# One core's attention and two MoE layers: a half-size group with two column tiles in a PSUM bank, and a new order for the first 30 microseconds

## The chip, the cores and the metric

The kernel runs on one core of a Trainium2 chip. A core has a matmul engine (TensorE, PE; the loading of its stationary operand is shown as PEld), VectorE (DVE), ScalarE (ACT), GpSimd (POOL, idle here), and SyncE (SP), whose queue issues every transfer of this kernel, in order. The metric is the time of one execution on the device, in microseconds (us).

## The reference

```python
scores = scale * np.matmul(q_c, k_c.transpose(0, 1, 2, 4, 3))       # chunks of 64, 8 heads of 64
attn = np.exp(scores - np.max(scores, axis=-1, keepdims=True))
attn = attn / (np.sum(attn, axis=-1, keepdims=True) + 1e-09)
x = heads_side_by_side(np.matmul(attn, v_c))                         # 4608 tokens x 512
a = x @ w1
b = x @ w2                                                           # 512 x 1024
x = (a * b @ w3) @ w_out                                             # w3: 1024 x 1024, w_out: 1024 x 512
h = x @ w_in                                                         # 512 x 2048
g = np.maximum(h, 0.0) + alpha * np.minimum(h, 0.0)                  # one alpha per column
out = g @ w_out2                                                     # 2048 x 512
```

`heads_side_by_side` stands for the reference's transpose and reshape. The weights of the two layers come as 64-bit floating-point numbers and are converted on the chip.

## The kernel before

Each fp32 operand is split into a high and a low half (`split`, HI and LO), and each product of 128x128 by 128 x columns is three matmuls, low by high, high by high and high by low (`PASSES`).

**Beginning.** Attention goes by units of 256 tokens (u = 0 to 17), two units to a block of 512 tokens (b). A unit has the steps S (scores, 64 small matmuls), M (max, two VectorE instructions), X (16 exponentials on ScalarE, eight for each of its two tiles), Y (sums and division on VectorE), T (8 transposes), P (ScalarE's copy `pt`), V (64 small matmuls into `pa`), c and d (high half of x by ScalarE, low half by VectorE). Each piece of a weight has A (ScalarE: absolute values), B (VectorE, 3 instructions), C (ScalarE's cast `wa`), D and E (VectorE, 2 each); the transfer that brings a piece is called `raw`, and piece n + 3 is asked for when piece n is done with its buffer. `a0.0` is the first product, block 0, column tile 0 of w1; k is ScalarE's copy of it out of PSUM, b the product with w2, m the multiplication of the two on VectorE. The string `STARTUP` is the order in which these steps are written; the framework's scheduler (`tile`) sets the order on each engine from it and from its own estimates, except for instructions given to `keep_in_program_order`. `LEAD = 4` blocks are worked in this stretch, and blocks 0 and 1 take turns first. Each product uses 12 matmuls of 512 columns.

**moe2's first product.** w_in's column tiles j = 0 to 7 are multiplied by operands that stand for x's parts in a scheme of seven products in place of eight (`ORDER`, `operand`). Tokens go in groups s (`wide = [512] * 4 + [256]`): four full-size groups and one of half size, in which every tile is 256 columns wide. A pass (s, j) works on two column tiles, j and j + 1, in the banks `a` and `b`, with a third pair of banks `bc` in turn. It has 14 products of 6 matmuls, in the order 4, 5, 3, 5, 0, 2, 6, 1 with two tiles each; ScalarE copies a bank out at three of them (`keep`: p1, u2, v), VectorE adds `bc` to these, and `leaky` makes the result: two relus on ScalarE, one multiply-add with alpha on VectorE, and a store to DRAM (`g2_dram`) from the buffer `r`. All copies and results take 128x512 buffers from one pool with `TMP = 7` slots. The weights of the second product (w_out2) are loaded into the places of those of the first as these are used for the last time, by the same queue as the stores.

**moe2's second product** ("q", "a", "b" from `op`) reads `g2_dram` back; its first matmuls need the banks a and b.

Of the kernel before, what the change touches and what calls it, by code (L numbers as in the profile page):

```python
# [18 lines left out]
P = 128  # L19
# [18 lines left out]
    S0 M0 X0 A0 S1 Y0 M1 T0 P0 B0 X1 V0 D0 c0 Y1 C0 A1 d0 T1 A2 E0 P1 S2 B1  # L38
    V1 A3 c1 M2 C1 d1 X2 D1 S3 B2 a0.0 M3 C2 Y2 X3 E1 T2 D2 b0.0 B3 P2 Y3 k0.0 V2
    C3 A4 m0.0 T3 c2 E2 P3 d2 a0.1 A5 D3 B4 V3 k0.1 E3 C4 c3 D4 b0.1 A6 d3 q4 q5 E4  # L40
    a1.0 m0.1 A7 B5 a0.2 k1.0 B6 C5 D5 C6 b1.0 D6 k0.2 E5 E6 A8 b0.2 m1.0 A9 B7 a1.1 m0.2 C7 D7
    B8 a0.3 k1.1 E7 C8 D8 A10 b1.1 k0.3 B9 E8 C9 b0.3 m1.1 A11 D9 B10 a1.2 m0.3 C10 E9 a0.4 k1.2 D10
    A12 B11 b1.2 k0.4 E10 C11 D11 A13 b0.4 m1.2 E11 B12 A14 a1.3 S4 m0.4 C12 D12 a0.5 M4 B13 k1.3 X4 E12
    C13 b1.3 D13 k0.5 A15 B14 E13 b0.5 C14 m1.3 S5 D14 M5 m0.5 E14 B15 Y4 X5 C15 D15 T4 P4 E15 a1.4
    A16 B16 k1.4 b1.4 C16 D16 E16 V4 Y5 q6 m1.4 a0.6 A17 B17 k0.6 b0.6 C17 D17 E17 T5 P5 V5 q7 m0.6
    a1.5 A18 B18 k1.5 b1.5 C18 D18 E18 m1.5 a0.7 A19 B19 k0.7 b0.7 C19 D19 E19 m0.7 a1.6 A20 B20 k1.6 b1.6 C20
    D20 E20 c4 d4 c5 d5 m1.6 a1.7 A21 B21 k1.7 b1.7 C21 D21 E21 S6 M6 X6 m1.7 a2.0 A22 B22 k2.0 b2.0
    C22 D22 E22 S7 M7 Y6 X7 m2.0 a2.1 A23 B23 k2.1 b2.1 C23 D23 E23 T6 P6 V6 c6 d6 m2.1 a2.2 A24
    B24 k2.2 b2.2 C24 D24 E24 Y7 T7 P7 V7 m2.2 a2.3 A25 B25 k2.3 b2.3 C25 D25 E25 c7 d7 m2.3 h0.0 A26
    B26 C26 D26 E26 h0.1 s0 w0 A27 B27 C27 D27 E27 a2.4 A28 B28 k2.4 b2.4 C28 D28 E28 m2.4 h1.0 A29 B29  # L50
    C29 D29 E29 a2.5 A30 B30 k2.5 b2.5 C30 D30 E30 m2.5 h1.1 s1 w1 a2.6 A31 B31 k2.6 b2.6 C31 D31 E31 m2.6
    h2.0 A32 B32 C32 D32 E32 a2.7 A33 B33 k2.7 b2.7 C33 D33 E33 m2.7 h2.1 s2 w2 A34 B34 C34 D34 E34 h3.0
    A35 B35 C35 D35 E35 a3.0 A36 B36 k3.0 b3.0 C36 D36 E36 m3.0 h3.1 s3 w3 a3.1 A37 B37 k3.1 b3.1 C37 D37
    E37 m3.1 h4.0 A38 B38 C38 D38 E38 a3.2 A39 B39 k3.2 b3.2 C39 D39 E39 m3.2 h4.1 s4 w4 a3.3 k3.3 b3.3 m3.3
    h5.0 h5.1 s5 w5 a3.4 k3.4 b3.4 m3.4 h6.0 a3.5 k3.5 b3.5 m3.5 h6.1 s6 w6 a3.6 k3.6 b3.6 m3.6 h7.0 a3.7 k3.7 b3.7
    m3.7 h7.1 s7 w7
# [7 lines left out]
TMP = 7  # L64


@with_exitstack
def tile_attention_moe_moe(ctx: ExitStack, tc: tile.TileContext, qkv: bass.AP, w12: bass.AP,
# [8 lines left out]
    nc = tc.nc  # L77
    NT, DM = out.shape
# [29 lines left out]
    def matmul(*args, **kw):  # L108
        ins = nc.tensor.matmul(*args, **kw)  # L109
        if pinned[0]:  # L110
            tc.keep_in_program_order(ins)

    def transpose(*args, **kw):
        ins = nc.tensor.transpose(*args, **kw)  # L114
        if pinned[0]:
            tc.keep_in_program_order(ins)

    def split(dst, src):

        nc.scalar.copy(dst[:, HI], src)  # L120
        nc.vector.tensor_tensor(out=dst[:, LO], in0=src, in1=dst[:, HI].bitcast(F32), op=ALU.subtract)  # L121
# [39 lines left out]
    def convert_a(i):  # L161
# [22 lines left out]
    def convert_c(i):
        nc.scalar.copy(w_g[conv[i]][:, HI], conv_m[i])

    def convert_d(i):

        p = conv_p[i] = tmp("p")
        nc.vector.tensor_scalar(out=p.bitcast(U32), in0=conv_m[i].bitcast(U32), scalar1=0xFF800000, scalar2=None,  # L190
                                op0=ALU.bitwise_and)
        nc.vector.scalar_tensor_tensor(out=p, in0=conv_raw[i][:, :, 0], scalar=2.0 ** -52, in1=p, op0=ALU.mult, op1=ALU.mult)

    def convert_e(i):
        m, g = conv_m[i], w_g[conv[i]]
        nc.vector.tensor_tensor(out=m, in0=m, in1=g[:, HI].bitcast(F32), op=ALU.subtract)  # L196
        nc.vector.tensor_tensor(out=g[:, LO], in0=m, in1=conv_p[i], op=ALU.add)
# [4 lines left out]
    def second_weight(i):  # L202
# [6 lines left out]
        nc.vector.tensor_tensor(out=m, in0=m, in1=conv_p.pop(i), op=ALU.add)  # L209

    def combined_weight(i):
# [14 lines left out]
        for out, x, y in ((t14[:, left], b12, b11), (t32[:, left], b22, b12), (t32[:, right], b22, t14[:, left]),  # L226
                          (t14[:, right], b21, t32[:, right])):
            nc.vector.tensor_tensor(out=out, in0=x, in1=y, op=ALU.subtract)
# [30 lines left out]
    def load_unit(u):  # L259
# [9 lines left out]
        v = un[u]["v"]  # L269
        for j in range(2):  # L270
            nc.sync.dma_start(out=un[u]["qk"][j], in_=qkv[2 * u + j, :, 0:2])
        for j in range(2):
# [16 lines left out]
    def attn_max(u):  # L289
        mx = un[u]["mx"] = work.tile([P, 2, 8], F32, tag="mx", name="mx")  # L290
        nc.vector.tensor_reduce(out=mx, in_=un[u]["s"].rearrange("p h (a k) -> p h a k", k=D), axis=AX.X, op=ALU.max)
        nc.vector.tensor_scalar_mul(mx, mx, -SCALE)  # L292

    def attn_exp(u, tiles=range(2)):
# [4 lines left out]
        for j in tiles:  # L299
            for a in range(4):  # L300
                for h2 in range(2):
                    n, h = 4 * j + a, h2 ^ (a & 1)
                    nc.scalar.activation(out=e[:, j, a, h], in_=s[:, h2, n * D:(n + 1) * D], func=AF.Exp,  # L303
                                         bias=mx[:, h2, n:n + 1], scale=SCALE, accum_out=sm[:, j, a, h:h + 1])

    def attn_softmax(u):
        e, sm = un[u]["e"].rearrange("p j a h k -> p (j a h) k"), un[u].pop("sm").rearrange("p j a h -> p (j a h)")
        nc.vector.tensor_scalar_add(sm, sm, 1e-9)
        nc.vector.reciprocal(sm, sm)
        nc.vector.tensor_tensor(out=e, in0=e, in1=sm.unsqueeze(2).to_broadcast([P, 16, D]), op=ALU.mult)  # L310
# [8 lines left out]
    def attn_copy(u):  # L319
        pt = un[u]["pt"] = work.tile([P, 2, 4, 2, D], F32, tag="pt", name="pt", bufs=1)  # L320
        nc.scalar.copy(pt.rearrange("p j a c s -> p j (a c s)"), un[u]["pa"])
# [13 lines left out]
    def attn_out(u, lo):  # L335
# [5 lines left out]
        if lo:  # L341
            nc.vector.tensor_tensor(out=xs[LO], in0=pa, in1=xs[HI].bitcast(F32), op=ALU.subtract)  # L342
            un.pop(u)
        else:
            nc.scalar.copy(xs[HI], pa)
# [15 lines left out]
    def fold_split(f, lo):  # L361
# [3 lines left out]
        if lo:  # L365
            nc.vector.tensor_tensor(out=dst[:, LO], in0=ps, in1=dst[:, HI].bitcast(F32), op=ALU.subtract)
        else:
            nc.scalar.copy(dst[:, HI], ps)
# [6 lines left out]
    def product(b, f, a, ps):  # L375
        nc.vector.tensor_tensor(out=a, in0=ps, in1=a, op=ALU.mult)
# [5 lines left out]
    def empty_pair(sums, last, name, to):  # L382

        for i in (last - 1, last):
            t = tmp(name)
            (nc.scalar.copy if i % 2 else nc.vector.tensor_copy)(t, sums[i])
# [53 lines left out]
    def add(out, x, y, op=ALU.add):  # L440
        nc.vector.tensor_tensor(out=out, in0=x, in1=y, op=op)  # L441
# [19 lines left out]
    def operand(o):  # L461
# [9 lines left out]
        nc.scalar.copy(h, x)  # L471
# [4 lines left out]
    for u in range(4):  # L476
        load_unit(u)
        if u < RAW:
            convert_load(u)
    nc.sync.dma_start(out=alpha_sb, in_=alpha)  # L480
    nc.vector.tensor_scalar_mul(nalpha, alpha_sb, -1.0)
    lent = {1: "p23", 3: "p23", 5: "p23", 7: "p23"}
    sets = 0
    for step in STARTUP.split():
        kind, rest = step[0], [int(n) for n in step[1:].split(".")]
        n = rest[0]
        if kind == "q":
# [3 lines left out]
        elif kind in "ST":  # L491
            {"S": attn_scores, "T": attn_transpose}[kind](n, lent.get(n, "att"))
        elif kind in "MXYPV":
# [11 lines left out]
        elif kind == "k":  # L505
            a = ab[tuple(rest)][2] = tmp("a")
            nc.scalar.copy(a, ab[tuple(rest)][0])  # L507
# [9 lines left out]


# [45 lines left out]
    for b in range(LEAD, NB):  # L564
        parts = [p for i in range(2) for p in unit_steps(2 * (b + 1) + i, False)] if b + 1 < NB else []
        for f in range(NF1):
# [5 lines left out]
            nc.scalar.copy(a, pa)  # L572
# [275 lines left out]
```

## Time and profile before

| | |
|---|---|
| time, median of 3 runs | 1462.27 us (1460.94 to 1463.52) |
| profiled execution | 1463.75 us, its span 1461.9 us |
| mean granted clock of TensorE | 0.995 |
| TensorE busy | 1411.9 us (97%) |
| VectorE busy | 1001.7 us (69%) |
| ScalarE busy | 737.5 us (50%) |
| the first product starts | 37.62 us |
| the half-size group, first matmul to the next stage's first | 1054.98 to 1105.42 us |

The profiled execution's time holds some 2 us outside the span, which runs from the first to the last instruction. Busy shares are means over the whole span. An engine's line in a timeline has its start, its duration, the operation with its output and inputs, how many of a kind stand in a row, and in brackets how long the engine had been idle and what released it.

### The profile page before, as it was taken

What the parts mean: (1) busy time and instruction counts of PE and PEld (TensorE: products, weight loads), DVE (VectorE), ACT (ScalarE), POOL (GpSimd) and SP (SyncE); (2) the same over time, 40 slices, a digit from 0 to 9 for tenths busy, and PEclk for the clock granted to TensorE, in tenths of its full rate; (3) what the DMA queues carried; (4) which work ended last, traced back from release to release, by engine and by line L of the source; (5) the groups of instructions that cost most, each with busy time, mean ns of one, the idle gap of its engine ahead of it and who ended that gap; (6) DMA issues with size and microseconds to landing.
All of it is one profiled execution on the core that took longest, in us unless ns stands there. A gap on an engine that the chain in (4) does not pass through costs nothing.

```text
span 1461.9 us, 22936 instructions
## 1 busy us (share of the span) xinstructions
PE 1411.9 (97%) x8608; PEld 1167.7 (80%) x8608; DVE 1001.7 (69%) x1533; ACT 737.5 (50%) x1603; POOL 0.7 (0%) x6
## 2 busy tenths in 40 slices
PE   4999999999999999999999999999999999999998
PEld 3777788887788888888878787878787888888887
DVE  4988786233487877776345758575756878888775
ACT  5545532144355545553247767686765444444433
POOL 0000000000000000000000000000000000000000
PEclk9999999999999999999999999999999999999999
DMA  8555342344466666668272424333589563745442
GB/s 260 188 188 168 108 157 95 131 151 148 141 216 217 216 216 220 218 221 304 91 273 108 148 112 158 116 137 116 177 277 324 188 216 116 210 136 176 144 140 89
DMA packets 132095, 256.32 MB, mean 175 GB/s; under 512 B 13712, under 2 KB 62864, under 8 KB 131984
## 3 DMA queue, kind: packets, MB, share of 16 engines
q1 hardware_dynamic: 131984, 254.87, 52.0%
q8 instruction: 67, 1.10, 0.3%
q14 instruction: 44, 0.36, 0.1%
HBM read 160.44 MB, written 94.37 MB: 174 GB/s over the span
## 4 chain that ended last, share of the span: by engine, by line
PE 83%; DVE 6%; ACT 5%; DMA 4%; issue 1%; SPq 0%; ACTq 0%; DVEq 0%
PE a L109 18%; PE b L109 18%; PE q L109 17%; PE acc L109 12%; PE bc L109 8%; PE ab L109 4%; PE wc L109 3%; ACT e L303 2%; DMA g_dram<-r 2%; PE sc L109 1%; PE pa L109 1%; DMA raw<-in_w 1%; PE pa L114 1%; DVE m L181 1%; DVE m L196 1%
## 5 line engine op out<-in xcount | busy, mean ns | idle before, releaser
L109 PE MATMUL q<-op,w 128*128 128x512 f32 (+1 forms) x1020 | 220.5, 369 | 2.2 <-DVE op L441 2.1
L109 PE MATMUL acc<-gs,wc 128*128 128x512 f32 x864 | 207.9, 393 | 3.4 <-DVE gs L121 3.1
L109 PEld LDWEIGHTS q<-op,w 128*128 128x128 f32 x1020 | 179.4, 190 | 34.4 <-DVE op L441 2.6
L109 PEld LDWEIGHTS acc<-gs,wc 128*128 128x128 f32 x864 | 160.3, 188 | 40.7 <-DVE gs L121 5.2
L109 PE MATMUL a<-x,wa 128*128 128x512 f32 x672 | 165.1, 394 | 0.4 <-DVE x L342 0.4
L109 PE MATMUL b<-x,wa 128*128 128x512 f32 x672 | 163.9, 392 | 0.0
L109 PEld LDWEIGHTS a<-x,wa 128*128 128x128 f32 x672 | 127.1, 190 | 27.1 <-DVE x L342 0.5
L109 PEld LDWEIGHTS b<-x,wa 128*128 128x128 f32 x672 | 124.8, 188 | 25.8
L109 PE MATMUL bc<-yo,w 128*128 128x512 f32 (+1 forms) x600 | 134.6, 368 | 0.0
L658 ACT CAST op<-araw 128x1024 fp32r<-128x1024 f32 (+1 forms) x80 | 77.3, 967 | 94.4 <-PE q L109 33.1
L109 PEld LDWEIGHTS bc<-yo,w 128*128 128x128 f32 x600 | 105.5, 189 | 18.7
L109 PE MATMUL b<-yo,w 128*128 128x512 f32 (+1 forms) x450 | 105.3, 369 | 1.7 <-ACT t L606 1.4
L441 DVE TENSOR_TENSOR op<-araw,op 128x1024 fp32r<-128x1024 f32 (+1 forms) x80 | 88.8, 1112 | 21.1 <-ACT op L658 20.5
L109 PE MATMUL ab<-x,wa 128*128 128x512 f32 x384 | 96.4, 400 | 4.9 <-ACT a L507 4.9
L109 PE MATMUL a<-yo,w 128*128 128x512 f32 (+1 forms) x390 | 92.1, 372 | 7.3 <-ACT p L619 5.0
L303 ACT ACTIVATE e<-sc,mx 128x64 f32<-128x64 f32 x288 | 86.2, 351 | 21.8 <-DVE mx L292 21.0
L109 PEld LDWEIGHTS b<-yo,w 128*128 128x128 f32 x450 | 79.1, 188 | 17.4 <-ACT t L606 3.0
L658 ACT CAST op<-sum 128x1024 fp32r<-128x1024 f32 (+1 forms) x60 | 58.0, 967 | 64.8 <-PE q L109 48.2
L109 PEld LDWEIGHTS ab<-x,wa 128*128 128x128 f32 x384 | 71.5, 190 | 23.2 <-ACT a L507 8.4
L109 PEld LDWEIGHTS a<-yo,w 128*128 128x128 f32 x390 | 68.3, 188 | 23.1 <-ACT p L619 6.6
L441 DVE TENSOR_TENSOR op<-sum,op 128x1024 fp32r<-128x1024 f32 (+1 forms) x60 | 66.6, 1109 | 28.1 <-ACT op L658 28.1
L303 ACT ACTIVATION_READ_ACCUMULATOR e<-sc,mx 128x1 f32 x288 | 70.1, 244 | 0.0
(121 smaller groups left out, 2075.6 us busy)
## 6 DMA issues: line engine op xcount, KB each, us to landing
araw<-g_dram SPq DMA_DIRECT2D x80, 512.0 KB, 3.9
g_dram<-r SPq DMA_DIRECT2D x128, 256.0 KB, 2.0
w_dram<-wm SPq DMA_DIRECT2D x48, 512.0 KB, 2.9
w<-w_dram SPq DMA_DIRECT2D x48, 512.0 KB, 4.9
qk<-in_qkv SPq DMA_DIRECT2D x36, 512.0 KB, 5.8
raw<-in_w2nd SPq DMA_DIRECT2D x32, 512.0 KB, 4.2
y_dram<-y SPq DMA_DIRECT2D x36, 256.0 KB, 2.8
raw<-in_w SPq DMA_DIRECT2D x16, 512.0 KB, 4.2
```

Source lines behind the costliest of these rows:

```text
L109: ins = nc.tensor.matmul(*args, **kw)
L114: ins = nc.tensor.transpose(*args, **kw)
L181: nc.vector.scalar_tensor_tensor(out=m.bitcast(U32), in0=conv_raw[i][:, :, 1], scalar=0xC0000000, in1=m.bitcast(U32), op0=ALU.bitwise_and, ...
L196: nc.vector.tensor_tensor(out=m, in0=m, in1=g[:, HI].bitcast(F32), op=ALU.subtract)
L303: nc.scalar.activation(out=e[:, j, a, h], in_=s[:, h2, n * D:(n + 1) * D], func=AF.Exp, bias=mx[:, h2, n:n + 1], scale=SCALE, accum_out=sm ...
L441: nc.vector.tensor_tensor(out=out, in0=x, in1=y, op=op)
L658: ins = nc.scalar.copy(out, x)
```

## The change

Two things. First, in the half-size group a pass works on four column tiles and not on two: each of the banks a, b and bc takes two tiles of 256 columns side by side, the group has two passes and not four, and copies, relus, adds and stores are 512 wide; the multiply-add with alpha stays 256 wide, since alpha differs by tile. Second, the beginning: q and k of units 0 and 1 and the first two weight pieces are asked for first, then v of these units, and after them the rest; an exponential on a single zero runs ahead of everything; the negated alpha is computed at the end of the beginning; and up to the mark `|` in `STARTUP`, which stands behind the first product, the three computing engines keep the written order (`InOrder`, `head`).

```diff
 STARTUP = """
-    S0 M0 X0 A0 S1 Y0 M1 T0 P0 B0 X1 V0 D0 c0 Y1 C0 A1 d0 T1 A2 E0 P1 S2 B1
+    S0 A0 M0 X0 B0 D0 S1 M1 C0 X1.0 Y0 A1 X1.1 E0 T0 B1 D1 P0 V0 Y1 c0 T1 C1 d0
...
+class InOrder:
+    def __init__(self, tc, engine, on):
+        self.tc, self.engine, self.on = tc, engine, on
+
+    def __getattr__(self, name):
+        f = getattr(self.engine, name)
+
+        def call(*args, **kw):
+            ins = f(*args, **kw)
+            if self.on[0]:
+                self.tc.keep_in_program_order(ins)
+            return ins
+        return call
...
+    head = [False]
+    vector, scalar = InOrder(tc, nc.vector, head), InOrder(tc, nc.scalar, head)
...
-        if pinned[0]:
+        if pinned[0] or head[0]:
             tc.keep_in_program_order(ins)
...
-    for u in range(4):
+    vector.memset(nalpha[:, 0:1], 0.0)
+    scalar.activation(out=nalpha[:, 0:1], in_=nalpha[:, 0:1], func=AF.Exp)
+    for u in range(2):
+        load_unit(u, False)
+        convert_load(u)
+    for u in range(2):
+        load_values(u)
+    convert_load(2)
+    for u in range(2, 4):
         load_unit(u)
-        if u < RAW:
-            convert_load(u)
     nc.sync.dma_start(out=alpha_sb, in_=alpha)
-    nc.vector.tensor_scalar_mul(nalpha, alpha_sb, -1.0)
+    head[0] = True
...
-    def leaky(s, j, q, h, t):
-        w, f = wide[s], j + NJ * (q % 2)
-        r = tmp("r")[:, :w]
-        nc.scalar.activation(out=r, in_=h, func=AF.Relu)
-        nc.scalar.activation(out=t, in_=h, func=AF.Relu, scale=-1.0)
-        nc.vector.scalar_tensor_tensor(out=r, in0=t, scalar=nalpha[:, f:f + 1], in1=r, op0=ALU.mult, op1=ALU.add)
-        nc.sync.dma_start(out=g2_dram[s, q, j // 2][:, j % 2], in_=r)
+    def leaky(s, js, q, h, t):
+        w, r = wide[s], tmp("r")[:, :h.shape[1]]
+        scalar.activation(out=r, in_=h, func=AF.Relu)
+        scalar.activation(out=t, in_=h, func=AF.Relu, scale=-1.0)
+        for i, j in enumerate(js):
+            f, at = j + NJ * (q % 2), slice(i * w, (i + 1) * w)
+            vector.scalar_tensor_tensor(out=r[:, at], in0=t[:, at], scalar=nalpha[:, f:f + 1], in1=r[:, at],
+                                           op0=ALU.mult, op1=ALU.add)
+        j = js[0]
+        to = g2_dram[s, q, j // 2]
+        nc.sync.dma_start(out=to[:, j % 2] if len(js) == 1 else to, in_=r if len(js) == 1 else r.rearrange("p (j c) -> p j c", j=2))
...
+    passes = []
+    for s, w in enumerate(wide):
+        n = TB // w
+        passes += [(s, j, [list(range(j + i * n, j + (i + 1) * n)) for i in range(2)]) for j in range(0, NJ, 2 * n)]
...
+        def both(i, o, ps, first, last):
+            w = wide[s]
+            for n, k in enumerate(jj[i]):
+                product(s, k, o, ps[:, n * w:(n + 1) * w], first and n == 0, last)
...
         for i in range(2):
-            product(s, jj[i], 4, a[i], True, False)
+            both(i, 4, a[i], True, False)
             p1[i] = keep("p1", i)
```

The other products of a pass change in the same way as the last one shown. What the change moves on the engines stands in their rows. First ScalarE, from the start of the program; before:

```order
L303 ACT_TABLE_LOAD
L303 ACTIVATE e,sm<-sc,mx 128x64 x16
L172 ACTIVATE m<-raw 128x512
L321 COPY pt<-pa 128x1024
L303 ACTIVATE e,sm<-sc,mx 128x64 x16
L345 CAST x<-pa 128x2x2x256
L185 CAST wa<-m 128x512
L172 ACTIVATE m<-raw 128x512 x2
L321 COPY pt<-pa 128x1024
L185 CAST wa<-m 128x512 x2
L303 ACTIVATE e,sm<-sc,mx 128x64 x3
L345 CAST x<-pa 128x2x2x256
```

and now:

```order
L77 ACT_TABLE_LOAD
L77 ACTIVATE nalpha<-nalpha 128x1
L77 ACTIVATE m<-raw 128x512
L77 ACTIVATE e,sm<-sc,mx 128x64 x16
L77 CAST wa<-m 128x512
L77 ACTIVATE e,sm<-sc,mx 128x64 x8
L77 ACTIVATE m<-raw 128x512
L77 ACTIVATE e,sm<-sc,mx 128x64 x8
L77 COPY pt<-pa 128x1024
L77 CAST x<-pa 128x2x2x256
L77 CAST wa<-m 128x512
L77 COPY pt<-pa 128x1024
```

The table load stands ahead of an exponential that needs no data, the first weight piece ahead of unit 0's exponentials, a weight's cast and its next piece ahead of and between unit 1's exponentials, and the first of unit 2's exponentials (the row x3 of before) no longer ahead of the high half of unit 1's x; they come four rows further on. TensorE from the start of the program (L109 and L114, and now L128 and L133, are the lines of the helpers for matmuls and transposes); before:

```order
L109 MATMUL sc<-qk 64x64 x64
L114 MATMUL pa<-ident,e 128x128 x8
L109 MATMUL pa<-pt,v 64x64 x32
L114 MATMUL pa<-ident,e 128x128 x8
L109 MATMUL sc<-qk 64x64 x32
L109 MATMUL pa<-pt,v 64x64 x32
L109 MATMUL sc<-qk 64x64 x32
L109 MATMUL a<-x,wa 128x512 x12
L109 MATMUL b<-x,wa 128x512 x6
```

and now:

```order
L128 MATMUL sc<-qk 64x64 x64
L133 MATMUL pa<-ident,e 128x128 x8
L128 MATMUL pa<-pt,v 64x64 x32
L133 MATMUL pa<-ident,e 128x128 x8
L128 MATMUL pa<-pt,v 64x64 x32
L128 MATMUL sc<-qk 64x64 x32
L128 MATMUL a<-x,wa 128x512 x12
L128 MATMUL sc<-qk 64x64 x32
```

The scores of unit 3 (the last `sc` row) stand behind the first product and no longer ahead of it, and both values steps ahead of unit 2's scores. Last, TensorE at the start of the half-size group; before:

```order
L109 MATMUL a<-yo,w_6802 128x256 x6
L109 MATMUL b<-yo,w_6880 128x256 x6
L109 MATMUL bc<-yo,w_6802 128x256 x6
L109 MATMUL a<-yo,w_6800 128x256 x6
L109 MATMUL b<-yo,w_6878 128x256 x6
L109 MATMUL bc<-yo,w_6880 128x256 x6
L109 MATMUL a<-yo,w_6798 128x256 x6
L109 MATMUL b<-yo,w_6876 128x256 x6
L109 MATMUL bc<-yo,w_6800 128x256 x6
```

and now:

```order
L128 MATMUL a<-yo,w_6804 128x256 x6
L128 MATMUL a<-yo,w_6882 128x256 x6
L128 MATMUL b<-yo,w_7215 128x256 x6
L128 MATMUL b<-yo,wx 128x256 x6
L128 MATMUL bc<-yo,w_6804 128x256 x6
L128 MATMUL bc<-yo,w_6882 128x256 x6
L128 MATMUL a<-yo,w_6802 128x256 x6
L128 MATMUL a<-yo,w_6880 128x256 x6
L128 MATMUL b<-yo,w_7213 128x256 x6
```

Each bank now takes 12 matmuls with two tiles' weights where it took 6, and comes round again after six rows and not after three.

## Rows read from the trace of the kernel before

**Rows 1.** Page, part 1: busy time and share of the span of each engine.

```profile
PE 1411.9 (97%) x8608; PEld 1167.7 (80%) x8608; DVE 1001.7 (69%) x1533; ACT 737.5 (50%) x1603; POOL 0.7 (0%) x6
```

**Rows 2.** Stretches: length, each engine's busy time, granted clock, DMA share, GB/s.

```profile
37.60:60.00 22.40, 21.77 (x215) 17.39 (x212) 20.03 (x38) 15.74 (x55) 0.00 (x0) 0.90 0.68 213
1035.94:1054.98 19.04, 19.04 (x85) 15.77 (x84) 14.48 (x22) 16.50 (x30) 0.00 (x0) 1.00 0.60 209
1054.98:1105.42 50.44, 43.96 (x337) 40.98 (x335) 30.60 (x63) 33.89 (x91) 0.00 (x0) 1.00 0.85 279
```

**Rows 3.** TensorE's timeline, first 58 us: start, duration, operation, idle before and releaser.

```profile
4.58 2.35 PE L109 MATMUL sc<-qk 64*64 64x64 f32 x64 [4.58 <-DMA qk<-in_qkv]
...
26.19 1.94 PE L114 MATMUL pa<-ident,e 128*128 128x128 f32 x8 [4.61 <-DVE e L310]
...
29.82 1.93 PE L109 MATMUL pa<-pt,v 64*64 64x64 f32 x64
35.70 1.99 PE L109 MATMUL sc<-qk 64*64 64x64 f32 x64 [3.95 <-DVE x L342]
37.62 5.00 PE L109 MATMUL a<-x,wa 128*128 128x512 f32 x12
...
52.44 3.02 PE L109 MATMUL ab<-x,wa 128*128 128x512 f32 x12
...
56.11 2.11 PE L109 MATMUL a<-x,wa 128*128 128x512 f32 x8 [0.39 <-DVE x L342]
```

**Rows 4.** ScalarE's timeline, first 58 us, same columns.

```profile
8.51 1.28 ACT L303 ACT_TABLE_LOAD   x1 [8.51 <-DVE mx L292]
...
14.45 0.75 ACT L172 ACTIVATE m<-raw 128x512 f32<-128x512 f32 x1
...
24.08 1.11 ACT L345 CAST x<-pa 128x1024 fp32r<-128x1024 f32 x1
...
28.22 1.01 ACT L321 COPY pt<-pa 128x1024 f32<-128x1024 f32 x1 [1.39 <-PE pa L114]
...
40.13 0.31 ACT L303 ACTIVATE e<-sc,mx 128x64 f32<-128x64 f32 x1 [1.29 <-DVE mx L292]
```

**Rows 5.** VectorE's timeline, first 58 us, same columns.

```profile
8.25 0.17 DVE L292 TENSOR_SCALAR mx<-mx 128x16 f32<-128x16 f32 x1
...
47.93 0.69 DVE L192 SCALAR_TENSOR_TENSOR p<-raw,p 128x512 f32<-128x512 uint32 x1
...
54.84 1.22 DVE L342 TENSOR_TENSOR x<-pa,x 128x1024 fp32r<-128x1024 f32 x1
```

**Rows 6.** TensorE's timeline in the half-size group.

```profile
1059.23 0.98 PE L109 MATMUL a<-yo,w 128*128 128x256 f32 x6 [1.94 <-ACT p L619]
...
1074.05 0.88 PE L109 MATMUL a<-yo,w 128*128 128x256 f32 x6
1074.77 0.88 PE L109 MATMUL b<-yo,w 128*128 128x256 f32 x6
...
1105.42 0.96 PE L109 MATMUL a<-op,w 128*128 128x512 f32 x3 [1.26 <-ACT t L606]
```

**Rows 7.** ScalarE's waits in the half-size group: total us, times, longest.

```profile
ACT v L619 <- DMA g_dram<-r: 3.1, 4, 1.3
```

**Rows 8.** ScalarE by shape, half-size group: busy us, mean ns, idle before.

```profile
L605 ACT ACTIVATE r<-p 128x256 f32<-128x256 f32 x8 | 3.3, 418 | 5.6 <-DVE p L441 5.3 <-DVE r L607 0.3
...
L619 ACT COPY p<-a 128x256 f32<-128x256 f32 x4 | 1.4, 351 | 0.0
```

**Rows 9.** The same of full-size groups, 960 to 1050 us.

```profile
L605 ACT ACTIVATE r<-p 128x512 f32<-128x512 f32 x10 | 6.3, 632 | 10.2 <-DVE p L441 10.0
...
L619 ACT COPY p<-a 128x512 f32<-128x512 f32 x5 | 2.9, 581 | 0.0
```

**Rows 10.** DMA issues in the half-size group: KB each, median us to landing.

```profile
w<-w_dram SPq DMA_DIRECT2D x13, 512.0 KB, 4.6
g_dram<-r SPq DMA_DIRECT2D x28, 128.0 KB, 3.4
```

More of the change, by code (lines that the diff above doesn't have):

```diff
@@ L208, in second_weight @@
         m = conv_m[i]
-        nc.vector.tensor_tensor(out=m, in0=m, in1=conv_p.pop(i), op=ALU.add)
+        vector.tensor_tensor(out=m, in0=m, in1=conv_p.pop(i), op=ALU.add)
     def combined_weight(i):
@@ L341, in attn_out @@
         if lo:
-            nc.vector.tensor_tensor(out=xs[LO], in0=pa, in1=xs[HI].bitcast(F32), op=ALU.subtract)
+            vector.tensor_tensor(out=xs[LO], in0=pa, in1=xs[HI].bitcast(F32), op=ALU.subtract)
             un.pop(u)
         else:
-            nc.scalar.copy(xs[HI], pa)
+            scalar.copy(xs[HI], pa)
     wc_g = {}
@@ L385, in empty_pair @@
             t = tmp(name)
-            (nc.scalar.copy if i % 2 else nc.vector.tensor_copy)(t, sums[i])
+            (scalar.copy if i % 2 else vector.tensor_copy)(t, sums[i])
             nc.sync.dma_start(out=to(i), in_=t)
@@ L470, in operand @@
         y_op[s, o] = h, l
-        nc.scalar.copy(h, x)
+        scalar.copy(h, x)
         add(l, x, h.bitcast(F32), ALU.subtract)
@@ L484, in tile_attention_moe_moe @@
     for step in STARTUP.split():
-        kind, rest = step[0], [int(n) for n in step[1:].split(".")]
-        n = rest[0]
-        if kind == "q":
+        kind, rest = step[0], [int(n) for n in step[1:].split(".") if n]
+        n = rest[0] if rest else 0
+        if kind == "|":
+            head[0] = False
+        elif kind == "q":
             load_unit(n)
@@ L492, in tile_attention_moe_moe @@
             {"S": attn_scores, "T": attn_transpose}[kind](n, lent.get(n, "att"))
+        elif kind == "X" and len(rest) > 1:
+            attn_exp(n, rest[1:])
         elif kind in "MXYPV":
@@ L506, in tile_attention_moe_moe @@
             a = ab[tuple(rest)][2] = tmp("a")
-            nc.scalar.copy(a, ab[tuple(rest)][0])
+            scalar.copy(a, ab[tuple(rest)][0])
         elif kind == "b":
@@ L617, in keep @@
         def keep(name, i):
-            t = tmp(name)[:, :w]
-            nc.scalar.copy(t, a[i])
+            t = tmp(name)
+            scalar.copy(t, a[i])
             return t
         def second(i):
-            n = 4 * NJ * s + j + i
-            bc = pair(("att", "p01", "p23")[n % 3], "bc")
-            b[i], c[i] = (bc[:, h, :w] for h in range(2))
-            product(s, jj[i], 5, b[i], True, True)
+            bc = pair(("att", "p01", "p23")[(2 * turn + i) % 3], "bc")
+            b[i], c[i] = (bc[:, h] for h in range(2))
@@ L657, in copied @@
     def copied(out, x):
-        ins = nc.scalar.copy(out, x)
+        ins = scalar.copy(out, x)
         if ordered[0]:
```

116 lines of the change are left out of this document (60 added, 56 removed).

## The prediction, on record before the changed kernel ran

> **What bounds the kernel now.** I read the page first: TensorE is busy 97% of the span [rows 1], so only places where it waits or runs slowly can give time back. I then took TensorE's waits and cut the span where they lie: the first 56 us, and the 50.44 us of the half-size group (the last 256 columns of moe2's first product). The full-size pass just before that group has no wait at all: 19.04 us long, TensorE busy 19.04 [rows 2]. That is 14 banks of six 512-column matmuls, 1.36 us each.
>
> In the half-size group the reader should see two things. A bank of six 256-column matmuls costs 0.72 us when nothing stalls (1074.05 to 1074.77) [rows 6], and there are 4 passes x 14 = 56 of them, so the matmuls alone are 40.32 us; the group takes 50.44 [rows 2]. The missing 10.1 us is waiting, named in the rows as "a <- ACT p" (1.94 at the first) and "a <- ACT t" (1.26 at the end) [rows 6]: TensorE wants to write a bank again, and ScalarE has not copied it out. ScalarE is not slow for want of rate: a copy of 256 columns costs 0.351 us and one of 512 costs 0.581, a relu 0.418 against 0.632 [rows 8, 9]. Most of the price of the narrow ones is paid per instruction. Per 256-column pass ScalarE has 6 copies and 16 relus, 6 x 0.351 + 16 x 0.418 = 8.8 us, against 10.08 us of matmuls: it fits on average, but not within the 2.16 us that three banks leave it.
>
> At the beginning TensorE waits for the first attention units. ScalarE stands idle until 8.51, loads its activation table for 1.28 us and only then starts the first exponentials [rows 4]. The scores of unit 3, which themselves waited 3.95 us for VectorE, and most of unit 2's exponentials stand ahead of the first product, which starts at 37.62 and needs 5.00 us for twelve matmuls, where a later set needs 3.02 [rows 3]. The granted clock of 37.6 to 60 is 0.90 [rows 2], so part of this stretch ran at the lower of its two levels (1.2 against 2.4 GHz). The next block's first product begins at 56.11, 0.39 us late, on VectorE's x [rows 3]. From there TensorE is fed well, and I count the beginning's gain at that point.
>
> **The half-size group, part by part.** Two column tiles share a bank, so the matmuls stay (336 of 128x256) and 2 passes of 14 double banks, 1.44 us each, replace 4 of 14: the floor stays 2 x 14 x 1.44 = 40.32 us. ScalarE's work per pass becomes 6 x 0.581 + 16 x 0.632 = 13.6 us [rows 9] against 20.16 us of matmuls, 67%; in the full-size pass, which has the same instructions, it is 13.6 of 19.04, or 71%, and TensorE does not wait there [rows 2]. The adds on VectorE halve in number; its multiply-adds with alpha stay 256 wide. So the pace should be that of the full-size pass, a little slacker.
>
> What is left over: at the entry the bank "a" is wanted again after three double banks, 4.32 us instead of 2.16, at about 1059.30, and the copy that TensorE waits for ended just before 1059.23 today [rows 6], because ScalarE is still working off the full-size pass. I take 0.2. At the exit the next product waits 1.26 for the last relu [rows 6]; the wider relus come later after their bank but TensorE also writes more after it, so I keep 1.26. Sum 41.8.
>
> The transfers: with the DMA share 0.85 over 50.44 us [rows 2], the queues hold 42.9 us of work, which is more than 41.8. The stores become 16 of 256 KB instead of 32 of 128 KB (28 of which are issued inside the stretch [rows 10]), which can only ease this, and loads for the next product can land later than the group's end, because only a quarter of the weights is wanted in its first microseconds. [...] Bounds: nothing (41.8) or all of it (42.9); I take the middle, 42.3. **Gain 8.1 us**, bounds 7.5 to 8.6 by these rows alone.
>
> The stores hold slots of the seven 128x512 buffers from which every copy is taken. A pass takes 16 of them: by my count of banks from each first write to its last read, the eight that keep p1, u2, v and t are held some 61 us in all (5.8, 8.7, twice 15.9, twice 5.8, twice 1.6), the eight results 2.2 us each plus the landing L of their store. Seven slots give 7 x 20.16 = 141 us; 61 + 17.6 + 8 L stays under that up to L = 7.8. The median now is 3.4 [rows 10]. No wait from this in the sum; ScalarE waits for such stores today (3.1 us in one kind of copy alone [rows 7]), so it is a rival.
>
> **The beginning.** The dummy exponential loads the table while nothing else runs. The rows show it from 8.51 to 9.79, between the max, ready at 8.42, and the first exponential [rows 4, 5], so 1.3 us leave the path. The Trainium skill ("ScalarE: Activation LUTs", section "What ACT_TABLE_LOAD costs") counts some 2.66 us for a switch, 1.28 for the load and 1.38 for a drain; the load agrees with the row, a drain does not appear in it. By the page the sum would be 1.4 us better.
>
> The new order, with the durations of before: scores end at 6.93 [rows 3]; max, as now, 8.42 [rows 5]; sixteen exponentials, 14.45 - 9.79 = 4.66 [rows 4], to 13.1; a weight's cast, taken as the 0.75 of the other 128x512 step [rows 4], 13.85; unit 1's exponentials with one more such step between, 19.3; copy 1.01, 20.3; values 1.93, 22.2; transposes 1.94, 24.2; copy 1.01, 25.2; values 1.93, 27.1; x's high half 1.11, 28.2; low half 1.22 [rows 3 to 5], 29.4; a tenth of a microsecond at some of these hand-overs: **29.8** for the first product, 7.8 us earlier than 37.62. The loads that it needs now stand first in SP's queue, which is why I add no wait for them.
>
> But little of it reaches 56.11. Behind the first product now come the exponentials of unit 2 and the scores of unit 3, which before stood ahead of it; the exponentials (4.66) fit beside the product. At the clock of before the product ends at 34.8; scores 1.99, 36.8; max 8.42 - 6.93 = 1.49, 38.3: unit 3's exponentials start 1.8 us before the 40.13 of today [rows 3 to 5]. From there the chain to the next block's product is as it was (copy, k, the product m, VectorE's weight step at 47.93, the load and cast behind it, x's low half at 54.84 [rows 5]). VectorE, 20.03 of 22.40 us busy here [rows 2], has a little less queued. I take **a gain of 2.0 us**, that product at 54.1. Bounds: if the first product ran at the clock of the later set, 3.02, two more; nothing, if VectorE's queue sets 56.11 anyway.
>
> **Sum.** 8.1 + 2.0 = 10.1. The profiled execution took 1463.75 us for a span of 1461.9; the median of the runs is 1462.27, 1.5 lower. So 1453.6 by the profiled one, and by the median **1452.1**, which I round to 1452.
>
> **Rivals.**
> 1. The beginning gives nothing back at the next block's product: VectorE's 89% [rows 2] speaks for it, its wait of only 0.39 us ahead of 56.11 [rows 3] too. 1462.3 - 8.1 = 1454.2.
> 2. The beginning gives 4: the first product runs fast. Against it speaks that the work ahead is as small and broken up as before. 1450.2.
> 3. The half-size group was paced by transfers and slots more than by narrow copies: ScalarE's waits for stores speak for it [rows 7], the full-size pass, with no wait at a share of 0.60 [rows 2], doesn't decide it, because the weights for the next product come in only during the small group. With half of the 10.1 us left, the group takes 45.4: gain 5.0, 1455.3.
> 4. TensorE stays at the lower clock longer. Its first product now follows more small work, and the stretch before the next block has three more sets of twelve; at 5.00 instead of 3.02 [rows 3] they cost 5.9 more, and the next block starts at 60.0, 3.9 late: 8.1 - 3.9 = 4.2, 1458.1. The Trainium skill ("TensorE: Matmul & The Clock Gate", Part 1) has the throttled state as the default, which activity releases; the 5.00 of the first set and the 3.02 of the later one agree.
> 5. The other side: SP's one queue, in order. The stores of the group stand behind weight loads, and such a load waits until TensorE has used the old weights for the last time; the two passes now free them in larger lots. A store that is late holds its slot, ScalarE waits, TensorE waits. It decides above L = 7.8; to eat all of the gain and 0.2% of the time beyond it (10.1 + 2.9, so a pass of 27.7 us) L would be about 14. 4.6 us is the load's median [rows 10]. At L = 15 the pass is (61 + 17.6 + 120) / 7 = 28.4, the group 56.8: 1466.7.
>
> **How the numbers follow.** Forecast 0.47 (its own range 1450.5 to 1453.5); rival 1: 0.15; rival 2: 0.11; rival 3: 0.14; rival 4: 0.07; rival 5: 0.04; the rest, 0.02, no change. The range leaves out rivals 4 and 5, the rest and the ends of 2 and 3: 1448.5 to 1457. What a measurement of this kernel can tell from no change is 0.2%, 2.9 us. Slower: rival 5, 0.04. Same: the rest and part of rival 4, where more slow sets would bring it over 1459.4, 0.05. Faster: 0.91.
>
> **What would show it.** In the trace of after: the half-size group some 42 us long, its waits "a <- ACT p" all but gone except at the entry, ScalarE's copies there at 0.58; first exponential near 8.5; first product near 30, twelve matmuls in about 5; the next block's near 54. I am wrong if the first product comes after 33 or that of the next block after 56, if stores in the group land in over 7 us, or if the DMA share there is at 1 with TensorE waiting behind it.

## The result, and the profile after

| | before | after |
|---|---|---|
| time, median | 1462.89 us (4 runs, 1460.94 to 1464.84) | 1448.17 us (4 runs, 1447.29 to 1451.04) |
| span of the profiled execution | 1461.9 us | 1446.4 us |
| first product starts | 37.62 us | 29.66 us |
| next block's product starts | 56.11 us | 53.72 us |
| half-size group starts | 1054.98 us | 1050.52 us |
| half-size group, length | 50.44 us | 40.31 us |
| from there to the end | 356.5 us | 355.6 us |

The ratio is 0.9901, with a 95% interval of 0.9884 to 0.9918: 14.7 us less, where 10 were forecast. The time lies 0.3 us under the range's lower end. Faster was right; the size was not.

In the profiled executions the 15.5 us between the spans fall into four places: 2.4 by the next block's product, 2.1 more between there and the half-size group, 10.1 in the group, 0.9 in the last 356 us.

The page of the changed kernel, part 1 (busy time and share of the span), beside [rows 1]:

```profile
PE 1404.0 (97%) x8608; PEld 1163.1 (80%) x8608; DVE 1001.3 (69%) x1522; ACT 731.0 (51%) x1560; POOL 0.7 (0%) x6
```

The half-size group of the changed kernel as a stretch, with the columns of [rows 2]:

```profile
1050.52:1090.83 40.31, 40.31 (x338) 40.31 (x336) 27.57 (x48) 27.85 (x47) 0.00 (x0) 1.00 0.93 321
```

TensorE is busy all of it: 56 x 0.72 = 40.32 was the floor, and this execution is at it. The DMA share went from 0.85 to 0.93 and the rate from 279 to 321 GB/s [rows 2], but the stretch is shorter: 12.92 MB passed in it and 14.06 MB in that of before, so about 1.1 MB landed outside it, and TensorE waited for none of this. TensorE's timeline of the changed kernel, where [rows 3, 6] had waits:

```profile
29.66 4.62 PE L128 MATMUL a<-x,wa 128*128 128x512 f32 x12 [2.60 <-DVE x L77]
34.21 1.16 PE L128 MATMUL sc<-qk 64*64 64x64 f32 x64
...
53.72 4.62 PE L128 MATMUL a<-x,wa 128*128 128x512 f32 x12 [1.89 <-DVE x L77]
...
100.36 3.01 PE L128 MATMUL ab<-x,wa 128*128 128x512 f32 x12 [1.76 <-ACT a L77]
...
1050.52 1.59 PE L128 MATMUL a<-yo,w 128*128 128x256 f32 x12
...
1054.83 1.60 PE L128 MATMUL a<-yo,w 128*128 128x256 f32 x12
```

Bank a comes round after 4.31 us, and TensorE does not wait at the entry (1.94 at that place in [rows 6]) nor at the exit (1.26 there). At the beginning the first product came at the forecast 29.8, and the next block's 0.4 earlier than the forecast 54.1. What I had not looked for stands at 100 us. The same place in TensorE's timeline of the kernel before:

```profile
102.20 4.53 PE L109 MATMUL ab<-x,wa 128*128 128x512 f32 x12 [2.61 <-ACT a L507]
```

There TensorE waited 2.61 us and then took 4.53 for twelve matmuls, part of them at the lower clock; now it waits 1.76 and takes 3.01.

### The profile page after: what moved, and what is told of

It reads as the page before. It is cut to its first block, busy times and chain, and to the rows that moved or that the text cites. A ratio compares the mean times of both kernels' runs of the same rounds, so it can differ in the third digit from the quotient of the medians.

```text
span 1446.4 us, 22817 instructions
## 1 busy us (share of the span) xinstructions
PE 1404.0 (97%) x8608; PEld 1163.1 (80%) x8608; DVE 1001.3 (69%) x1522; ACT 731.0 (51%) x1560; POOL 0.7 (0%) x6
## 3 DMA queue, kind: packets, MB, share of 16 engines
q1 hardware_dynamic: 129680, 254.87, 52.1%
## 4 chain that ended last, share of the span: by engine, by line
PE 87%; ACT 5%; DVE 4%; DMA 3%; issue 1%; SPq 0%; ACTq 0%; DVEq 0%
PE a L128 19%; PE b L128 19%; PE q L128 17%; PE acc L128 13%; PE bc L128 9%; PE ab L128 4%; PE wc L128 3%; ACT e L77 3%; DVE m L77 1%; PE sc L128 1%; PE pa L128 1%; DVE p L77 1%; DMA g_dram<-r 1%; DMA raw<-in_w 1%; PE pa L133 1%
## 5 line engine op out<-in xcount | busy, mean ns | idle before, releaser
L128 PE MATMUL q<-op,w 128*128 128x512 f32 (+1 forms) x1020 | 219.6, 368 | 3.3 <-DVE op L77 3.3
L128 PE MATMUL acc<-gs,wc 128*128 128x512 f32 x864 | 207.7, 393 | 3.1 <-DVE gs L77 2.8
L128 PEld LDWEIGHTS q<-op,w 128*128 128x128 f32 x1020 | 178.6, 188 | 35.5 <-DVE op L77 3.7
L128 PEld LDWEIGHTS acc<-gs,wc 128*128 128x128 f32 x864 | 160.2, 188 | 40.3 <-DVE gs L77 4.9
L128 PE MATMUL a<-x,wa 128*128 128x512 f32 x672 | 166.3, 396 | 4.5 <-DVE x L77 4.5
L128 PE MATMUL b<-x,wa 128*128 128x512 f32 x672 | 163.7, 392 | 0.0
L128 PEld LDWEIGHTS a<-x,wa 128*128 128x128 f32 x672 | 127.9, 191 | 31.6 <-DVE x L77 4.8
L128 PEld LDWEIGHTS b<-x,wa 128*128 128x128 f32 x672 | 124.8, 188 | 25.9
L128 PE MATMUL bc<-yo,w 128*128 128x512 f32 (+1 forms) x600 | 133.6, 368 | 0.0
L128 PEld LDWEIGHTS bc<-yo,w 128*128 128x128 f32 x600 | 105.1, 189 | 18.7
L128 PE MATMUL b<-yo,w 128*128 128x512 f32 (+1 forms) x450 | 103.9, 369 | 1.0 <-ACT t L77 1.0
L128 PE MATMUL ab<-x,wa 128*128 128x512 f32 x384 | 95.1, 395 | 4.6 <-ACT a L77 4.2
L128 PE MATMUL a<-yo,w 128*128 128x512 f32 (+1 forms) x390 | 90.6, 370 | 3.5 <-ACT p L77 2.2
L128 PEld LDWEIGHTS b<-yo,w 128*128 128x128 f32 x450 | 78.7, 189 | 16.2 <-ACT t L77 2.3
L128 PEld LDWEIGHTS ab<-x,wa 128*128 128x128 f32 x384 | 70.6, 188 | 22.7 <-ACT a L77 7.9
L77 ACT COPY a<-a 128x512 f32<-128x512 f32 x56 | 33.4, 597 | 105.4 <-PE a L128 100.6
L77 DVE TENSOR_SCALAR m<-m 128x512 f32<-128x512 f32 (+1 forms) x144 | 60.5, 423 | 35.8 <-ACT m L77 35.0
```

The lines of the kernel that those rows point to most:

```text
L77: ins = f(*args, **kw)
```

## The experiments

Times are medians; each ratio is to the kernel before, measured beside it. Of every profiled execution three places are compared: the next block's product, the end of TensorE's last wait for a product's copy, which every kernel has, and the length of the half-size group. That wait, before and after:

```profile
252.44 3.01 PE L109 MATMUL ab<-x,wa 128*128 128x512 f32 x12 [0.19 <-ACT a L507]
248.69 3.02 PE L128 MATMUL ab<-x,wa 128*128 128x512 f32 x12 [0.19 <-ACT a L77]
```

| kernel | time, us | ratio (95%) | next block's product | wait ends | group |
|---|---|---|---|---|---|
| before | | | 56.11 | 252.44 | 50.44 |
| after | 1448.17 | 0.9901 (0.9884 to 0.9918) | 53.72 | 248.69 | 40.31 |
| after_again | 1448.83 | 0.9905 (0.9888 to 0.9921) | 52.99 | 246.23 | 40.82 |
| half_only | 1453.63 | 0.9929 (0.9917 to 0.9941) | 56.48 | 254.87 | 40.86 |
| start_only | 1458.93 | 0.9968 (0.9956 to 0.9981) | 53.63 | 246.64 | 51.21 |
| narrow_ops | 1448.84 (one run) | | 53.44 | 248.35 | 41.59 |
| two_stores | 1448.44 (one run) | | 54.15 | 248.84 | 41.02 |
| narrow_all | 1444.94 (one run) | | 52.93 | 246.01 | 40.75 |
| no_preload | 1446.90 | 0.9891 (0.9877 to 0.9905) | 53.10 | 247.35 | 40.97 |
| old_loads | 1451.35 | 0.9918 (0.9905 to 0.9931) | 54.93 | 249.01 | 41.67 |
| free_order | 1448.11 | 0.9896 (0.9877 to 0.9916) | 54.32 | 248.91 | 41.41 |
| warm | 1449.59 | 0.9901 (0.9887 to 0.9916) | 54.49 | 246.20 | 41.65 |
| c3_first | 1447.33 | 0.9886 (0.9869 to 0.9904) | 52.14 | 246.04 | 41.99 |
| before_warm | 1465.20 | 1.0016 (1.0004 to 1.0028) | 56.36 | 252.00 | 52.01 |

**The two halves apart.** half_only is the changed kernel with the old beginning:

```diff
-    S0 A0 M0 X0 B0 D0 S1 M1 C0 X1.0 Y0 A1 X1.1 E0 T0 ...
+    S0 M0 X0 A0 S1 Y0 M1 T0 P0 B0 X1 V0 D0 c0 Y1 C0 ...
...
-    head[0] = True
```

with the old loads as well.

> The kernel before with the half-size group's change alone. Theory (the group's gain is its own, the beginning's gain is the beginning's): group 40.3 us instead of 50.44 and nothing else, so 10.1 to 11 us less than before, 1452 to 1453; the next block's first product stays near 56.1 and the wait at 102 us stays 2.6. Rival (the group went down to its floor only because the new beginning put the queue of transfers in another phase): group over 41.5 us, gain under 9.

start_only is the changed kernel with the old passes:

```diff
-    for turn, (s, j, jj) in enumerate(passes):
+    for s, j in [(s, j) for s in range(len(wide)) for j in range(0, NJ, 2)]:
```

and the old `leaky`.

> The kernel before with the new beginning alone, half-size group as before. Theory: next block's first product near 53.7 (2.4 earlier), wait at about 100 us 1.8 instead of 2.6 and no stretch at the lower clock behind it, so 3.7 earlier from 120 us on, 4 to 5 us less than before in all, 1457.5 to 1459. Rival (what came after 56 us is scatter between executions and not the beginning's): 2 to 2.5 us less, 1460.5.

The group went to 40.86 without the new beginning and stayed at 51.21 without its own change, so its gain is its own; 9.6 us in the medians, a little under the 10.1 to 11 expected here. 0.71% and 0.32% add up to 1.03%, against 0.99% for both: the halves add. start_only gives 4.3 to 4.7 us, the larger of the two forecasts.

**What frees TensorE in the group: the width of the operations, or the way round?** narrow_ops puts ScalarE's work back to 256 columns, two operations for each double bank:

```diff
-            scalar.copy(t, a[i])
+            for at in parts_of(jj[i]):
+                scalar.copy(t[:, at], a[i][:, at])
```

and the relus in the same way.

> The changed kernel, but in the half-size group ScalarE's copies and relus are 256 columns wide again, two for each double bank; banks, adds and stores stay as in the changed kernel. Theory (the price per instruction was the bound): ScalarE needs 17.6 us of the 20.16 of a pass instead of 13.6, TensorE waits again, group 42.5 to 45 us. Rival (what helped is that a bank comes round half as often, the width of the operations matters little): group 40.3 to 41.

narrow_all narrows VectorE's adds and the stores too.

> The changed kernel with everything behind TensorE in the half-size group 256 wide again (copies, relus, adds, stores, two for each double bank), so that only the order of the products is new: a bank comes round after 4.32 us instead of 2.16. Theory now, after the run with narrow copies and relus (41.6 us): the longer way round is what helps; group 41 to 42.5 us. Rival (the wide operations together do): 45 us or more, towards the 50.4 of before.

two_stores splits only the stores:

```diff
-        nc.sync.dma_start(out=to[:, j % 2] if len(js) == 1 else to, in_=r if len(js) == 1 else r.rearrange("p (j c) -> p j c", j=2))
+        for i, j in enumerate(js):
+            nc.sync.dma_start(out=to[:, j % 2], in_=r[:, i * w:(i + 1) * w])
```

> The changed kernel with each store of the half-size group split into two of 128 KB. Theory (transfers don't bound the group): group 40.3 to 41 us, though the DMA share goes from 0.93 to about 1. Rival (coarser stores made the transfers fit): TensorE waits for relus that wait for stores, group 42.5 us or more.

41.59, 40.75 and 41.02 us all lie among the lengths that the group with wide operations had in eight executions, 40.31 to 41.99. The theory that a price per instruction bounded the group falls, though the ranges named for the way round were missed a little too (41.59 against 40.3 to 41, 40.75 against 41 to 42.5), and in two_stores the DMA share was 0.91 where about 1 was expected. All three are single executions. The stretch of narrow_all:

```profile
1048.56:1089.31 40.75, 40.56 (x338) 40.36 (x336) 28.55 (x58) 30.72 (x88) 0.00 (x0) 1.00 0.92 303
```

ScalarE is busy 30.72 us, only 2.9 more than with half as many operations. I had summed durations; but one operation begins before the last has ended, as ScalarE's timeline of the kernel before shows:

```profile
1058.83 0.35 ACT L619 COPY p<-a 128x256 f32<-128x256 f32 x1
1059.08 0.37 ACT L619 COPY p<-b 128x256 f32<-128x256 f32 x1
```

The second starts 0.25 us after the first, not 0.35. The Trainium skill ("ScalarE: Activation LUTs", section "What ACT_TABLE_LOAD costs") says that back-to-back ACTIVATEs overlap by about 93 ns; these rows, which are copies, have 100.

What the change gives is the way round, and two things come round half as often in all three kernels: a bank, and a buffer of the pool, which now holds two tiles and not one. For the bank speaks the entry of the group. ScalarE's timeline of the changed kernel, and then its waits for stores in the group:

```profile
1053.87 0.57 ACT L77 COPY p<-a 128x512 f32<-128x512 f32 x1
```

```profile
ACT r L77 <- DMA g_dram<-r: 3.3, 2, 1.8
```

The copy of bank a began 3.35 us after the bank's first matmul, too late for a bank wanted again after 2.16, in time for one wanted after 4.31. For the buffers speaks that ScalarE waited for stores 6.8 us in all, in ten waits, in the group of before ([rows 7] has the largest kind), and 3.3 in two waits now; in narrow_all it was 2.5 in three. No run changes the one without the other, so what share each has is not shown.

**The table.** no_preload leaves the dummy exponential out:

```diff
-    vector.memset(nalpha[:, 0:1], 0.0)
-    scalar.activation(out=nalpha[:, 0:1], in_=nalpha[:, 0:1], func=AF.Exp)
```

> The changed kernel without the exponential on a single zero. Theory: the table is loaded ahead of the first real exponential or ahead of the first weight step, 1.3 us on the way to the first product if it stands behind the max and nothing if it stands ahead of the weight step, which waits for its data until 7.7 anyway; first product 29.7 to 31.0, next block's product 53.7 to 55.0, time 0 to 1.3 us more than the changed kernel. Rival (the preload is worth the 2.7 us of load and drain): over 2 us more.

ScalarE's first rows in no_preload:

```profile
0.73 1.28 ACT L77 ACT_TABLE_LOAD   x1 [0.73 <-PEq L884]
7.62 0.66 ACT L77 ACTIVATE m<-raw 128x512 f32<-128x512 f32 x1 [5.61 <-DMA raw<-in_w]
```

The load stands at 0.73 all the same, ahead of the first operation that ScalarE has, which is now the absolute values of a weight. In half_only, where X0 is written first as in the kernel before, it stands at 8.49. So the 1.28 us left the path with A0's place ahead of X0; the dummy is worth nothing that was measured.

**The loads, and the fixed order.** old_loads has the loads in the order of before, all else new:

```diff
-    for u in range(2):
-        load_unit(u, False)
-        convert_load(u)
-    for u in range(2):
-        load_values(u)
-    convert_load(2)
-    for u in range(2, 4):
+    for u in range(4):
         load_unit(u)
+        if u < RAW:
+            convert_load(u)
```

> The changed kernel with the loads in the order of before (q, k, v and weight piece of unit 0, then of unit 1, and so on). Theory (the loads' order is what lets the new order run): unit 1's scores wait for their data until 11.8 as before instead of 9.0, and the first weight piece comes after 10, ahead of which ScalarE's fixed order lets no exponential run; first product 33 to 35, next block's product 56 or later, time 2 to 4 us more than the changed kernel. Rival (the loads are early enough either way): within 1 us.

Its rows, of ScalarE and then of TensorE:

```profile
10.97 0.66 ACT L77 ACTIVATE m<-raw 128x512 f32<-128x512 f32 x1 [8.74 <-DMA raw<-in_w]
```

```profile
32.80 4.61 PE L128 MATMUL a<-x,wa 128*128 128x512 f32 x12 [2.47 <-DVE x L77]
```

The first product is 3.1 us later, the next block's 1.2 to 1.9, earlier than the 56 expected. The time is 2.5 us more in the medians than after_again's, beside which it ran, which would be about half of the beginning's gain; the two intervals overlap, so the size is not shown. free_order lets the scheduler decide (`head[0] = True` removed).

> The changed kernel with the new loads and the new written order, but without the fixed order up to the first product: the scheduler decides. Theory (the loads and the place of the first weight step carry the gain, fixing the order a part of it): first product 31 to 36, next block's product 53.5 to 56, time 0 to 2.5 us more than the changed kernel. Rival (the fixed order is the whole of it): next block's product at 56 or later and 4 us more.

The first product came at 31.21, 1.6 later; the time, 1448.11, is that of the changed kernel. The fixed order is not what carries the gain.

**What sets the next block's product.** warm puts twice eight idle matmuls into TensorE's gaps ahead of the first product:

```diff
+        elif kind == "Z":
+            idle = bank("b")
+            w = w_g["a", 0, 0]
+            for i in range(n):
+                matmul(idle, w[:, HI, :P], w[:, HI], start=True, stop=True)
```

> The changed kernel with twice eight idle matmuls (128x512, into a bank that isn't in use yet) in TensorE's gaps at 17 and 27 us, so that it comes to the first product busier. Theory (the first product's pace does not set the next block's): the first product's twelve matmuls may take 3 us instead of 4.6, but the next block's product still begins at 53.5 to 54, since units 2 and 3's exponentials and the load and cast behind them set it; time within 1 us of the changed kernel, less only by what a fuller clock saves later. Rival (what TensorE loses at the lower clock is on the path): next block's product at 52 to 52.5, 1.5 to 2 us less.

The first product took 3.02 instead of 4.62, and the next block's came at 54.49, not earlier. But warm had a slow stretch of its own on the way, as TensorE's timeline shows:

```profile
44.58 1.99 PE L128 MATMUL pa<-pt,v 64*64 64x64 f32 x64 [2.80 <-ACT pt L77]
```

The same 64 matmuls took 1.16 in the changed kernel (at 47.25). Kernels with the same beginning say more: where the first product took 3.01 or 3.02 (after_again, start_only, narrow_all), the next block's came at 52.93 to 53.63, and where it took 4.23 to 4.62 (no_preload, narrow_ops, the changed kernel, two_stores), at 53.10 to 54.15. So the first product's pace is worth some half a microsecond there, not the two of the rival. after_again is the same kernel once more.

> The changed kernel itself, unchanged, for more executions. If the part of the gain that came after 56 us (some 1.3 us up to 120 us and 0.9 in the last 40) is from fewer stretches at the lower clock, its executions show a higher mean granted clock than those of the kernel before (0.997 to 0.999 against 0.993 to 0.997), and within each kernel the faster executions are those of the higher clock. If it is scatter, both kernels show the same clocks on average.

Its mean clock was higher than that of the kernel before beside it, 0.9988 against 0.9955. Within it the order did not hold: its slowest execution, 1452.18, had 0.998, and one of 1449.20 had 0.997.

c3_first keeps the high half of unit 3's x ahead of the next weight step in ScalarE's queue. ScalarE's rows of the changed kernel show why it was tried:

```profile
50.84 0.66 ACT L77 ACTIVATE m<-raw 128x512 f32<-128x512 f32 x1 [2.05 <-DMA raw<-in_w]
51.41 1.00 ACT L77 CAST x<-pa 128x1024 fp32r<-128x1024 f32 x1
```

The cast's input was there; it stood behind an operation that waited 2.05 us for a load.

```diff
-    ... k0.1 E3 C4 c3 D4 b0.1 A6 d3 q4
+    ... k0.1 E3 < C4 c3 A6 > D4 b0.1 d3 q4
```

(`<` and `>` fix ScalarE's order between them.)

> The changed kernel, but on ScalarE the high half of unit 3's x is kept ahead of the absolute values of the seventh weight piece, for whose load it waited 2.05 us (48.8 to 50.84) with x queued behind it. Theory (this wait in ScalarE's queue sets the next block's product): unit 3's x at 48.8 to 49.8 instead of 51.4, next block's product at 51.5 to 52, as TensorE comes free, 1 to 2 us less than the changed kernel, about 1447.5. Rival (VectorE's queue sets it): next block's product at 53 or later, time as before.

Now in c3_first, ScalarE and then TensorE:

```profile
49.05 1.01 ACT L77 CAST x<-pa 128x1024 fp32r<-128x1024 f32 x1
```

```profile
52.14 2.11 PE L128 MATMUL a<-x,wa 128*128 128x512 f32 x8
```

The product follows the work ahead of it without a wait, 0.85 us earlier than in after_again, which ran at the same clock, and 1.6 than in the changed kernel's first profile. So the wait in the queue was what set it. The time, 1447.33, is the lowest of the timed versions but one, and its interval overlaps the changed kernel's: better than before for certain, than the change not shown.

**The clock.** before_warm is the kernel before with ten idle matmuls in the gap ahead of unit 3's scores, all other orders the same (the lines of warm, with `V1`, the idle ones and `S3` in fixed order).

> The kernel before with nothing changed but ten idle matmuls (128x512, into a bank that isn't in use yet) in TensorE's gap at 31.8 to 35.7 us; the order of all other work is the same. Theory (a part of the change's gain, by its executions' clocks some 2 to 3 us, is that its executions hold fewer stretches at the lower clock): the first product's twelve matmuls take 3 us instead of 5.0, the mean granted clock of the executions rises from 0.995 to 0.997 or more, time 1 to 2.5 us less than before. Rival (the whole of the beginning's gain is the order of the work): the clock may rise, but the time stays within 0.7 us of before.

Its rows of TensorE:

```profile
30.86 2.56 PE L109 MATMUL b<-wa 128*128 128x512 f32 x10
...
36.69 4.60 PE L109 MATMUL a<-x,wa 128*128 128x512 f32 x12
```

The idle matmuls ran at the full level (0.23 us each), then TensorE stood still for 2.18 us, and the first product ran at the lower level again for a part of its 4.60. The mean granted clock of its executions was 0.9969 against 0.9961 for the kernel before beside it, and the time 0.16% more, some 2.3 us. Theory and rival both missed: the run doesn't say what a fuller clock would give. Up to the wait at 252.00 nothing is lost; from there to the half-size group it took 805.11 us, where the kernel before took 802.54 and all others but warm (804.22) 801.6 to 802.9, and the group took 52.01 instead of 50.44. Why is not settled.

## Why the prediction was wrong

**The half-size group: right, for half a reason.** 42.3 was forecast and 40.31 came, in eleven executions 40.3 to 42.0; the gain was 9.6 by half_only, not 8.1. Of the three remainders that I added to the floor, none has to appear: the entry's 0.2 and the exit's 1.26 are in some executions (the sum of TensorE's waits behind ScalarE is 2.0 in c3_first, none in the changed kernel; in after_again 1.68 come at the second bank of the next stage, just behind the group as it is measured here), and the DMA's "42.9 us of work" was no bound: 0.93 x 40.31 = 37.5 of it stood in the shorter stretch, and the rest moved out, as "loads for the next product can land later than the group's end" had allowed. The term was mis-sized by up to 2 us. The argument from widths, "most of the price of the narrow ones is paid per instruction", is wrong: narrow_all has every narrow operation and keeps the gain. The other half of the same sentence, that ScalarE's work does not fit "within the 2.16 us that three banks leave it", agrees with narrow_all. Rival 3 (transfers and slots) is out by two_stores as far as the transfers go, since stores of 128 KB as before cost nothing; the slots are not out, since every kernel with the gain has two tiles in a slot. The prediction's own count of slots, done for the kernel before with all times halved but the landing, gives a limit of L = 3.9 as an estimate, where the median was 3.4 [rows 10] and the longest landing 4.6. So the old group stood near that limit, which the prediction did not work out. Rival 5 did not come: the stores landed in 4.5 us at the median, 6.2 at most, under the 7.8 of the count of slots.

**The beginning: the step that failed is "From there TensorE is fed well, and I count the beginning's gain at that point".** The sum for the first product held (29.8 against 29.66), with some luck in its last links: in the changed kernel unit 1's values took 1.16 and not 1.93, and x's low half then stood in VectorE's queue behind weight steps until 28.39, though the high half was ready at 27.21; the chain had no such wait. The size of what reaches the next block held too (2.0 against 2.4).

But the gain grew behind that point. In the first pair of profiles the set at 53.72 ran partly at the lower level (4.62), that at 56.11 of the kernel before did not, so at their ends only 0.8 of the 2.4 was left (58.18 against 58.96); behind the waits at 100 us it was 3.4, and by the wait near 250 us it is 3.75. It differs between executions: 246.0 to 246.6 in the four executions of the new order with a mean clock of 1.00 in those 250 us, 252.0 to 254.9 in the three of the old order. Old and new order with about the same clock there, 0.99, stand at 252.0 (before_warm) and 248.7 (after): 3.3 us, which is more than the 2.4 at the next block's product.

A part of the rest goes with the clock. Over the timed executions the mean granted clock was 0.9946 to 0.9961 for the kernel before (four series, 45 executions in all) and 0.9989 for the changed one (9), and in the series beside half_only the slower executions of the kernel before are those of the lower clock (1465.9 at 0.993, 1461.5 at 0.997). But the clock is not all of it: with the same 0.99 on the way there, warm reached the wait at 246.20, no_preload at 247.35 and the changed kernel at 248.69. Nor does the length of a wait alone say whether the clock falls. At 100 us the wait of 2.61 had a stretch at the lower level behind it and the one of 1.76 none, but in narrow_ops and then no_preload, at the same place, it is the other way round:

```profile
98.47 4.39 PE L128 MATMUL ab<-x,wa 128*128 128x512 f32 x12 [1.78 <-ACT a L77]
98.97 3.03 PE L128 MATMUL ab<-x,wa 128*128 128x512 f32 x12 [2.62 <-ACT a L77]
```

That the new order causes the higher clock was argued and not shown: half_only, with the old beginning, had 0.9960 and start_only 0.9968, against 0.9948 for the kernel before beside them, and before_warm, which should have shown it, did not raise the clock where it was meant to. Rival 2 came nearest in size (4 us; start_only has 4.3 to 4.7). Its reason, a faster first product, is not the next block's start, but it isn't out: the five executions of the new order whose first product took 3.01 to 3.03 reached the wait near 250 us at 246.0 to 246.6, the six with 4.2 to 5.1 at 247.4 to 249.0. No run tells whether the first product's pace does this or what comes with it. So the step that failed is known, and by how much; what makes up the 1.9 to 2.3 us behind the next block's product stays open in part.

**Smaller steps.** The 1.3 us of the table load left the path, by the place of a weight step and not by the dummy. The bound "nothing, if VectorE's queue sets 56.11 anyway" named the wrong queue: it was ScalarE's, by a wait for a load (c3_first). Rival 1 fell with start_only, rival 4 too: the lower clock came for single sets (4.62 us at 29.66 and at 53.72) and went.

## What to carry to other kernels

If an engine waits to write a buffer again, count the time between two uses of the buffer before the price of what empties it: more work between the uses can be enough, with the same instructions. And see what else the new order holds longer or less often, here the buffers of the pool, before one of the two is named as the cause. When an early part of a kernel gets shorter, look for the gain at the last wait that the part touches, and not at the first place that is fed again. Before an operation is put ahead of others to hide a setup, see where the setup stands without it.

## What the runs showed of the hardware

One operation of ScalarE starts before the one ahead of it has ended (0.25 us from start to start where each lasts 0.35 to 0.37), so a sum of durations overstates its load: 88 operations cost 30.72 us of busy time where 47, of which most do twice as much, cost 27.85. The executions of one and the same kernel differ by up to 7 us here (1458.95 to 1465.88 for the kernel before beside before_warm). A part of it goes with stretches at TensorE's lower level, a part does not: at the same mean granted clock, 0.995, that kernel took 1460.66 to 1465.88. The changed kernel reached the wait near 250 us at 248.69 in one execution and 246.23 in another, whose granted clock over those 250 us was 0.99 and 1.00.
